# Value and state products issued by half units, and one shared pool for the weight conversions' words and temporaries

## The chip, the cores and the metric

The kernel runs on one core of one Trainium2 chip. Its time is the device time of an execution in microseconds (us). TensorE (PE in the profile; PEld is its weight load) multiplies, VectorE (DVE) and ScalarE (ACT) do the elementwise work and empty PSUM, GpSimd (POOL) does a little, and SyncE (SP) issues nearly all DMA transfers. Each engine works through its own instructions in the order in which they were written.

## The reference, cut to what matters

Three stages follow one another: a linear attention with complex decay, a soft mixture of experts over its output, and a feed-forward layer.

```python
for t in range(S):                          # 768 positions, 4 x 8 heads, head_dim 48
    new_re = ar * S_re - ai * S_im          # a normalised to modulus <= 0.999
    new_im = ar * S_im + ai * S_re
    S_re, S_im = new_re + k[:, :, t] (x) v[:, :, t], new_im
    y[:, :, t] = einsum('bhd,bhde->bhe', q[:, :, t], S_re)
...
logits = x @ phi                            # x: 3072 tokens x 384, 32 slots
slot_input = softmax(logits, 0).T @ x       # over the tokens
h = maximum(slot_input[e] @ w1[e], 0); slot_out[e] = h @ w2[e]      # 8 experts, 384 -> 1024 -> 384
x = softmax(logits, 1) @ slot_out
...
h = x @ w_in                                # 384 -> 2048 -> 384
out = maximum(0.01 * h, h) @ w_out
```

## The kernel before, in words

**Attention.** The work is cut into 12 units: 6 chunks of 128 positions by 2 pairs of batch entries. A unit has 16 heads in two halves (one batch entry each), and four quarters `hq` of 4 heads. Per unit, logarithms, sines and exponentials of the decay are computed (`prep1` to `prep3`, `decay`; their sums over positions are the matmuls of L572), and `prep4` (L625, L634) scales q and k on DVE. Then `attend` writes five steps per quarter:

- `mA` (L649) transposes q and k on PE into a bank of `btr`; ACT or DVE copies them to `qt` and `kt` (L655, L653).
- `mB` (L664) makes the scores in a bank of `bsc`; DVE multiplies them by the causal mask into a tile of `sc` (L667; `sc` has 2 tiles).
- `mC` (L689) adds up scores times v and, from chunk 1 on, q times the carried state `S`, into one bank of `bm` per half. Its matmuls stand in pairs, one writing output partitions 0 to 63 and one 64 to 127. One call covers a quarter: 8 matmuls, or 4 in chunk 0.
- `mD` (L707) makes the quarter's contribution to the state in another bank of `bm`; after the second quarter DVE adds it to `S` and multiplies by the decay (L721, L722; in chunk 0 one instruction, L719). Chunk 5 has no `mD`.
- `mE` copies y out (ACT L730), transposes it (PE L734) and copies it again (ACT L738).

After each chunk, `slots` (L754 to L788) computes the logits and a running softmax sum `acc` over the tokens.

**Experts.** w1 and w2 come as 64 slabs of 384 KB. 49 of them go to tiles of the pool `w`, the others to tiles of other pools that attention has left. `layer1` (L931) and `layer2` (L967) use 32 slabs each, in two groups of experts (`gr`); a group of `layer2` ends with an ACT copy (L974), three transposes (L978) and small DVE copies (L986). `product` (L1004 to L1019) multiplies the result by w_in. A slab can be loaded into a tile of `w` when the earlier owner's last reader is done, and SP issues in order.

**Conversions.** w_in and w_out come as 64-bit floats; `conv` loads a piece of 384 KB into a tile of `raw`, and ACT (L447) and DVE (L448 to L451) narrow it to 32 bits through a tile of `tmp`. There are 16 pieces of w_in and 16 of w_out. For w_out two more instructions split the result (L479, L480).

**Feed-forward.** `ffn1` (L1029 to L1033) and `ffn2` (L1046 to L1048, 1152 matmuls) run to the end.

**What sets the order.** Every step is handed to a planner (`Plan`) with a list of tiles and a cost in us written by hand. The planner simulates the engines with these costs, the pools' numbers of tiles and a few waiting rules, and emits the instructions of each engine in the order that it found. So a changed cost or pool size can move any instruction on any engine.

Of the kernel before, what the change touches and what calls it, by code (L numbers as in the profile page):

```python
# [12 lines left out]
I32 = mybir.dt.int32  # L13
AF = mybir.ActivationFunctionType
ALU = mybir.AluOpType
# [3 lines left out]
B, H, S, D = 4, 8, 768, 48  # L19
# [5 lines left out]
P = 128  # L25
# [3 lines left out]
W = G * D  # L29
# [269 lines left out]
def c_dve(n):  # L299
    return 0.069 + 1.04e-3 * n  # L300
# [19 lines left out]
def tile_kernel(  # L320
# [14 lines left out]
    V, A, GP, T, SY = nc.vector, nc.scalar, nc.gpsimd, nc.tensor, nc.sync  # L335
# [147 lines left out]
    st = [dict() for _ in range(NU)]  # L483
# [154 lines left out]
                    [(q, o), (cs, 0, o), (cs, 1, o)], [d],  # L638
                )

    qt, sc, yb, ub, xt, yt = {}, {}, {}, {}, {}, {}

    def mA(u, hq):
        for nm, tg in (("q", t_qt), ("k", t_kt)):
# [13 lines left out]
    def mB(u, hq):  # L658
        b, t = b_sc(), t_sc([P, 4, P])
        k, q = qt[u, hq, "k"], qt[u, hq, "q"]  # L660

        def mm():
            for i in range(4):
                T.matmul(b()[:, P * i:P * i + P], lhsT=k()[:96, i, :], rhs=q()[:96, i, :], start=True, stop=True)  # L664

        pe(0.88, mm, [k, q], [b])
        dve(c_dve(512), lambda: V.tensor_tensor(t(), b().rearrange("p (i t) -> p i t", t=P), tri.unsqueeze(1).to_broadcast([P, 4, P]), op=ALU.mult), [b], [t])  # L667
        sc[u, hq] = t

    def mC(u, hq):  # L670
        c, bp = divmod(u, 2)
        v = st[u]["v"]
        if hq % 2 == 0:
            yb[u] = b_m()
        y, t, q = yb[u], sc[u, hq], qt[u, hq, "q"]

        def mm():
            for pr in range(2):
                o = P * (2 * (hq % 2) + pr)
                for kind in range(2 if c else 1):  # L680
                    for j in range(2):
                        i = 2 * pr + j
                        g = 4 * hq + i
                        m = 64 if j == 0 and kind == 0 else 48
                        if kind == 0:
                            l, r = v()[:, D * g:D * g + m], t()[:, i, :]
                        else:
                            l, r = sbuf[bp]()[:, D * g:D * g + m], q()[:96, i, :]
                        T.matmul(y()[64 * j:64 * j + m, o:o + P], lhsT=l, rhs=r, start=kind == 0, stop=kind == 1 or c == 0)  # L689

        pe(0.88 if c else 0.44, mm, [t, q, v, (sbuf[bp], hq // 2)], [y])

    def mD(u, hq):
        c, bp = divmod(u, 2)
        if c == NCH - 1:
            return
        s = st[u]
        if hq % 2 == 0:
            ub[u] = b_m()
        b, k, v = ub[u], s["k", hq], s["v"]  # L700

        def mm():
            for i in range(4):
                g = 4 * hq + i
                o = D * (g % 8)
                n = D
                T.matmul(b()[:96, o:o + n], lhsT=k()[:, i].rearrange("p t d -> p (t d)"), rhs=v()[:, D * g:D * g + n], start=True, stop=True)  # L707

        pe(0.68, mm, [k, v], [b])
        if hq % 2 == 1:  # L710
            h = hq // 2
            dc = s["dc"]
            sl = lambda: sbuf[bp]()[:, 8 * D * h:8 * D * h + 8 * D]
            s3 = lambda: sl().rearrange("p (g e) -> p g e", e=D)
            key = (sbuf[bp], h)
            dcb = lambda: dc()[:96, 8 * h:8 * h + 8].unsqueeze(2).to_broadcast([96, 8, D])
            rd = [(dc, 0), (dc, 1)]
            if c == 0:
                dve(c_dve(384), lambda: V.tensor_tensor(s3(), b()[:96, :8 * D].rearrange("p (g e) -> p g e", e=D), dcb(), op=ALU.mult), [b] + rd, [key])  # L719
            else:  # L720
                dve(c_dve(384), lambda: V.tensor_tensor(sl(), b()[:96, :8 * D], sl(), op=ALU.add), [b], [key])  # L721
                dve(c_dve(384), lambda: V.tensor_tensor(s3(), s3(), dcb(), op=ALU.mult), rd, [key])  # L722

    def mE(u, h):
        c, bp = divmod(u, 2)
        bi = 2 * bp + h
        y, b = yb[u], b_m()
        t = yt[c, bi] = t_yt()
        x = xt[c, bi] = t_x()
        act(512, lambda: A.activation(t()[:112], y()[:112, :], AF.Copy), [y], [t])  # L730

        def tr():
            for pr in range(4):
                T.transpose(b()[:, 112 * pr:112 * pr + 112], t()[:112, P * pr:P * pr + P], ident[:112, :112])  # L734

        pe(0.44, tr, [t], [b])
        for j in range(2):
            act(192, lambda j=j: A.activation(  # L738
                x().rearrange("p (r j e) -> p r j e", j=2, e=D)[:, :, j, :],
                b()[:, 0:448].rearrange("p (r w) -> p r w", w=112)[:, :, 64 * j:64 * j + D], AF.Copy), [b], [(x, j)])  # L740

    phi_mm = None

    def slots(c):
# [3 lines left out]
        b, e, lg = (b_sc if last else b_m)(), t_dd(), t_dd()  # L748
        ts = [yt[c, i] for i in range(4)]
# [6 lines left out]
        phi_mm = pe(0.86, mm, ts, [b])  # L756
        m0, m1, n1 = mx[:, c:c + 1], mx[:, c + 1:c + 2], nm[:, c + 1:c + 2]
        dve(0.2, lambda: V.tensor_reduce(m1, b()[:, :P], axis=AX.X, op=ALU.max), [b], [("mx", c + 1)])
        if c:
# [28 lines left out]
            dve(0.2, lambda: V.tensor_reduce(den, e(), axis=AX.X, op=ALU.add), [e], ["den"])  # L788

    def attend(u):  # L790
        for hq in range(4 + 3):
            if hq < 4:
                mA(u, hq)
            if 0 <= hq - 1 < 4:
                mB(u, hq - 1)
            if 0 <= hq - 2 < 4:
                mC(u, hq - 2)
                mD(u, hq - 2)
                if hq % 2 == 1:
                    mE(u, (hq - 2) // 2)  # L800

    turns, done, sel = [], set(), {}

# [347 lines left out]
```

## Time and profile before

| what | value |
|---|---|
| median of 3 runs | 520.32 us (520.12 to 520.55) |
| the profiled execution's own time | 519.7 us |
| its span, first to last instruction | 517.8 us |
| PE busy in the span | 486.8 us (94%), 3985 matmul records |
| DVE busy | 335.4 us (65%) |
| ACT busy | 361.9 us (70%) |
| mean DMA rate | 129 GB/s, 66.97 MB |

The profile is of one execution. A matmul of 32-bit floats appears as two records, and a matmul's record is longer than the distance to the next one, because matmuls overlap. What a run of matmuls costs is therefore read from starts, or from the pieces of the chain of work that ended last. Busy shares are averages over stages with different limits, so the rows further down are given by stage.

### The profile page before, as it was taken

The page shows a single profiled execution, that of the slowest core. Times are in us where ns is not written, and L with a number is a line of the kernel's source. Part 1 is how long each engine was busy: PE and PEld are TensorE (multiplying, and loading weights), DVE is VectorE, ACT ScalarE, POOL GpSimd, SP SyncE. Part 2 cuts the span into 40 slices and gives each one's busy share as a digit, 9 for nine tenths or more (in the row PEclk, how much of TensorE's full clock was granted, in tenths as well). Part 3 has the DMA queues.
Part 4 walks back from the last instruction along what each step waited for, and adds up shares of the span by engine and source line. Part 5 has one row for each costly group of instructions (what it writes and reads, how often), then busy time and mean ns, then how long its engine had stood idle before and what let it go on. Part 6 is the DMA issues. An engine that isn't in the chain of part 4 may idle for free.

```text
span 517.8 us, 10312 instructions
## 1 busy us (share of the span) xinstructions
PE 486.8 (94%) x3985; PEld 433.6 (84%) x3985; DVE 335.4 (65%) x705; ACT 361.9 (70%) x702; POOL 12.7 (2%) x27
## 2 busy tenths in 40 slices
PE   2598979999999999999898999999999999999997
PEld 1387768888889889878553899999999999999997
DVE  4677999999899998997851999825320443025130
ACT  7898999899899999675321799439830994069332
POOL 1000000000000000001000000000000000000000
PEclk9997989999999999999899999999999999999999
DMA  7955245525614746599797234300100110010102
GB/s 266 335 201 154 76 139 155 170 78 154 186 43 143 213 133 231 203 306 305 233 363 308 75 113 121 92 32 17 46 1 0 47 46 1 1 46 2 46 1 91
DMA packets 43844, 66.97 MB, mean 129 GB/s; under 512 B 19098, under 2 KB 24970, under 8 KB 43796
## 3 DMA queue, kind: packets, MB, share of 16 engines
q1 hardware_dynamic: 43476, 66.29, 39.1%
q8 instruction: 31, 0.51, 0.4%
q0 software_dynamic: 320, 0.03, 0.1%
q14 instruction: 17, 0.14, 0.1%
HBM read 61.53 MB, written 4.75 MB: 128 GB/s over the span
## 4 chain that ended last, share of the span: by engine, by line
PE 77%; ACT 9%; DMA 6%; DVE 6%; issue 1%; SPq 0%; POOL 0%; ACTq 0%; DVEq 0%; POOLq 0%
PE b L1047 13%; PE b L1048 13%; PE b L1046 13%; PE btr L649 7%; PE bm L689 6%; PE bsc L664 6%; PE bc L572 5%; PE b L1029 4%; PE bm L707 4%; DMA w<-in_w_dram 3%; ACT L186 2%; DMA raw<-in_wo_dram 1%; PE bm L734 1%; DMA raw<-in_wi_dram 1%; PE b L931 1%
## 5 line engine op out<-in xcount | busy, mean ns | idle before, releaser
L1033 DVE TENSOR_TENSOR w<-x,w 128x384 fp32r<-128x384 f32 x128 | 68.5, 555 | 109.5 <-ACT w L1032 109.5
L1047 PE MATMUL b<-w 128*128 128x384 f32 x384 | 129.2, 337 | 0.3 <-DVE w L1033 0.3
L1046 PE MATMUL b<-w 128*128 128x384 f32 x384 | 128.8, 335 | 0.0
L1048 PE MATMUL b<-w 128*128 128x384 f32 x384 | 128.5, 335 | 0.0
L1032 ACT ACTIVATE w<-x 128x384 fp32r<-128x384 f32 x128 | 63.3, 528 | 19.6 <-PE b L1048 18.4
L1047 PEld LDWEIGHTS b<-w 128*128 128x128 f32 x384 | 72.1, 188 | 0.6 <-DVE w L1033 0.6
L1046 PEld LDWEIGHTS b<-w 128*128 128x128 f32 x384 | 72.1, 188 | 0.0
L1048 PEld LDWEIGHTS b<-w 128*128 128x128 f32 x384 | 72.1, 188 | 0.0
L1031 ACT ACTIVATE x<-b 128x384 f32<-128x384 f32 x128 | 58.8, 491 | 8.6 <-DVE w L1033 5.2
L664 PE MATMUL bsc<-qt,kt 96*128 96x128 f32 x384 | 50.8, 277 | 1.6 <-DVE kt L653 1.0
L1055 ACT ACTIVATE k<-b 128x384 f32<-128x384 f32 x24 | 11.4, 484 | 54.8 <-PE b L1048 54.6
L664 PEld LDWEIGHTS bsc<-qt,kt 96*128 96x128 f32 x384 | 46.2, 192 | 3.2 <-DVE kt L653 1.3
L689 PE MATMUL bm<-sc,w 128*64 128x128 f32 (+1 forms) x384 | 37.4, 281 | 0.3 <-ACT x L738 0.3
L667 DVE TENSOR_TENSOR sc<-bsc,tri_r 128x512 f32<-128x512 f32 x48 | 32.8, 684 | 4.4 <-PE bm L689 2.4
L707 PEld LDWEIGHTS bm<-w,k 128*96 128x96 f32 x320 | 30.9, 167 | 3.2 <-issue 2.2
L707 PE MATMUL bm<-w,k 128*96 128x48 f32 x320 | 33.2, 250 | 0.0
L186 ACT ACT_TABLE_LOAD x25 | 32.1, 1283 | 1.2 <-PEq L1140 0.8
L655 ACT ACTIVATE qt<-btr 96x512 f32<-96x512 f32 x48 | 28.4, 592 | 6.3 <-PE btr L649 5.5
L649 PE MATMUL btr<-ident,q 128*96 128x128 f32 x192 | 30.8, 284 | 1.4 <-DVE q L634 0.8
L689 PE MATMUL bm<-qt,S 96*48 96x128 f32 x320 | 31.2, 272 | 0.0
L649 PE MATMUL btr<-ident,k 128*96 128x128 f32 x192 | 29.9, 281 | 1.1 <-ACT kt L655 0.8
L689 PEld LDWEIGHTS bm<-sc,w 128*64 128x64 f32 (+1 forms) x384 | 21.4, 129 | 8.1 <-issue 4.5
(173 smaller groups left out, 791.8 us busy)
## 6 DMA issues: line engine op xcount, KB each, us to landing
w<-in_w_dram SPq DMA_DIRECT2D x49, 384.0 KB, 5.0
w<-in_qkv_dram SPq DMA_DIRECT2D x36, 384.0 KB, 5.5
w<-in_a_dram SPq DMA_DIRECT2D x22, 384.0 KB, 4.8
raw<-in_wi_dram SPq DMA_DIRECT2D x16, 384.0 KB, 3.3
raw<-in_wo_dram SPq DMA_DIRECT2D x16, 384.0 KB, 3.1
out_dram<-k SPq DMA_DIRECT2D x24, 192.0 KB, 1.8
cs<-in_w_dram SPq DMA_DIRECT2D x6, 384.0 KB, 5.4
k<-in_w_dram SPq DMA_DIRECT2D x6, 192.0 KB, 3.8
```

Of the source, the lines that this page charges most:

```text
L186: self.preload(TABLES[name])
L649: T.transpose(b()[:96, P * i:P * i + P], src()[:, i].rearrange("p t d -> p (t d)"), ident)
L664: T.matmul(b()[:, P * i:P * i + P], lhsT=k()[:96, i, :], rhs=q()[:96, i, :], start=True, stop=True)
L667: dve(c_dve(512), lambda: V.tensor_tensor(t(), b().rearrange("p (i t) -> p i t", t=P), tri.unsqueeze(1).to_broadcast([P, 4, P]), op=ALU.mu ...
L689: T.matmul(y()[64 * j:64 * j + m, o:o + P], lhsT=l, rhs=r, start=kind == 0, stop=kind == 1 or c == 0)
L707: T.matmul(b()[:96, o:o + n], lhsT=k()[:, i].rearrange("p t d -> p (t d)"), rhs=v()[:, D * g:D * g + n], start=True, stop=True)
L1031: act(NG, lambda: A.activation(u(), b()[:, :NG], AF.Prelu, alpha=0.01), [b], [u])
L1032: act(NG, lambda: A.activation(g()[:, 0], u(), AF.Copy), [u], [(g, 0)])
L1033: dve(c_dve(NG), lambda: V.tensor_tensor(g()[:, 1], u(), g()[:, 0].bitcast(F32), op=ALU.subtract), [u, (g, 0)], [(g, 1)])
L1046: T.matmul(b()[:, :DM], lhsT=lh, rhs=wh()[:, i], start=f == FO[0], stop=False)
L1047: T.matmul(b()[:, :DM], lhsT=ll, rhs=wh()[:, i], start=False, stop=False)
L1048: T.matmul(b()[:, :DM], lhsT=lh, rhs=wl()[:, i], start=False, stop=f == FO[-1])
```

## The change

`mC` and `mD` are called once per half unit in place of once per quarter, so that 16 (chunk 0: 8) and 8 matmuls stand in one step that the planner can't cut. `mD` writes to a bank of `bsc` in place of `bm`. The costs given to the planner are new (2.0 and 1.13 for `mC`, 1.36 for `mD`, 1.15 for the logits' matmuls). The pools `raw` and `tmp` with 2 tiles each are gone, their users take tiles of `w`, and `w` has 33 tiles in place of 29; the memory taken is the same.

```diff
-    t_w = Tag(mem, "w", [P, W], 29)
+    t_w = Tag(mem, "w", [P, W], 33)
...
-    t_raw = Tag(mem, "raw", [P, W // 2, 2], 2, I32)
-    t_tmp = Tag(mem, "tmp", [P, 2, W // 2], 2)
...
     def conv(src, i, dst):
 
-        raw = t_raw()
+        raw = t_w([P, HW, 2], I32)
...
-        tmp = t_tmp()
+        tmp = t_w([P, 2, HW])
...
-    def mC(u, hq):
+    def mC(u, h):
+
         c, bp = divmod(u, 2)
-        v = st[u]["v"]
-        if hq % 2 == 0:
-            yb[u] = b_m()
-        y, t, q = yb[u], sc[u, hq], qt[u, hq, "q"]
+        v, hs = st[u]["v"], (2 * h, 2 * h + 1)
+        y = yb[u] = b_m()
...
-        pe(0.88 if c else 0.44, mm, [t, q, v, (sbuf[bp], hq // 2)], [y])
...
+        pe(2.0 if c else 1.13, mm, [x for hq in hs for x in (sc[u, hq], qt[u, hq, "q"])] + [v, (sbuf[bp], h)], [y])
...
-        if hq % 2 == 0:
-            ub[u] = b_m()
-        b, k, v = ub[u], s["k", hq], s["v"]
+        b, v, ks = b_sc(), s["v"], [s["k", 2 * h + j] for j in range(2)]
...
-        pe(0.68, mm, [k, v], [b])
...
+        pe(1.36, mm, ks + [v], [b])
...
     def attend(u):
-        for hq in range(4 + 3):
+        for hq in range(5):
             if hq < 4:
                 mA(u, hq)
-            if 0 <= hq - 1 < 4:
+            if hq:
                 mB(u, hq - 1)
-            if 0 <= hq - 2 < 4:
-                mC(u, hq - 2)
-                mD(u, hq - 2)
-                if hq % 2 == 1:
-                    mE(u, (hq - 2) // 2)
+            if hq in (2, 4):
+                mC(u, hq // 2 - 1)
+                mD(u, hq // 2 - 1)
+                mE(u, hq // 2 - 1)
```

**TensorE, behind the second chunk's slot sums** (at 116 us in the trace of before). `sc` are masked scores, `w` is v, `qt` is q, `S` the state; the numbers tell tiles apart. Before:

```order
L777 MATMUL bm_1409<-x_1365,dd_1399 32x384
L689 MATMUL bm_1420<-sc_1300,w_609 64x128
L689 MATMUL bm_1420<-sc_1300,w_609 48x128
L689 MATMUL bm_1420<-qt_1178,S_396 48x128 x2
...
L649 MATMUL btr_1434<-ident_60,q_1385 96x128 x4
L649 MATMUL btr_1439<-ident_60,k_1401 96x128 x4
L689 MATMUL bm_1420<-sc_1363,w_609 64x128
L689 MATMUL bm_1420<-sc_1363,w_609 48x128
L689 MATMUL bm_1420<-qt_1193,S_396 48x128 x2
```

The same place now:

```order
L771 MATMUL bm_1412<-x_1300,dd_1405 32x384
L688 MATMUL bm_1420<-sc_1357,w_578 64x128
L688 MATMUL bm_1420<-sc_1357,w_578 48x128
L688 MATMUL bm_1420<-qt_1188,S_396 48x128 x2
...
L688 MATMUL bm_1420<-sc_1379,w_578 64x128
L688 MATMUL bm_1420<-sc_1379,w_578 48x128
L688 MATMUL bm_1420<-qt_1247,S_396 48x128 x2
...
L662 MATMUL bsc_1446<-qt_1364,kt_1369 128x128 x4
```

The two transposes that stood between the two quarters' products have moved behind them. Over the whole program, matmuls of `mC` stand in 41 runs before (4 of 4, 32 of 8, 5 of 16 matmuls) and in 24 now (4 of 8, 20 of 16); of chunks 1 to 5 alone, in 35 and 20. Runs of `mD` go from 34 to 20.

**SyncE, the last loads before the feed-forward.** `in_w_dram` are slabs, `in_wi_dram` and `in_wo_dram` pieces to convert. Before:

```order
L352 DMA x<-in_w_dram 128x384 x3
L352 DMA raw<-in_wi_dram 128x768
L352 DMA raw<-in_wo_dram 128x768
L352 DMA w<-in_w_dram 128x768 x20
L352 DMA raw<-in_wo_dram 128x768 x15
```

Now:

```order
L352 DMA qt<-in_w_dram 128x384 x2
L352 DMA x<-in_w_dram 128x384 x3
L352 DMA w<-in_w_dram 128x768 x16
L352 DMA w<-in_wo_dram 128x768 x16
```

Four slabs have moved ahead of the last run of slabs, the last piece of w_in has moved up among the earlier loads, and the first piece of w_out has moved behind the slabs.

**TensorE, the end of the experts' second layer.** Before:

```order
L967 MATMUL b<-k,h_91 32x384 x3
L967 MATMUL b<-qt,h_91 32x384
L978 MATMUL b<-ident,x 128x128 x3
L967 MATMUL b<-w,h_91 32x384 x16
L978 MATMUL b<-ident,x 128x128 x3
```

Now:

```order
L960 MATMUL b<-k,h_91 32x384 x3
L960 MATMUL b<-qt,h_91 32x384
L960 MATMUL b<-w,h_91 32x384 x8
L971 MATMUL b<-ident,x 128x128 x6
```

The transposes of the first group of experts no longer stand ahead of the last matmuls of the second group, and half of those 16 matmuls stand earlier.

On VectorE, conversion instructions (L448 to L451) ahead of the last unit's phase step (L584 there, L582 now) go from 36 to 48 of the 64 for w_in; the other 16 follow before the feed-forward in place of 28.

## Rows read from the trace of the kernel before

**Rows 1.** Head of the page.
```profile
span 517.8 us, 10312 instructions
```

**Rows 2.** Windows: stretch and length, busy us (instructions) per engine, clock, DMA.
```profile
66.00:216.00 150.00, 147.29 (x1525) 126.39 (x1524) 141.29 (x264) 137.94 (x224) 6.03 (x8) 0.99 0.49 151
216.00:255.12 39.12, 35.56 (x405) 29.27 (x405) 35.19 (x93) 24.52 (x52) 2.63 (x6) 1.00 0.84 277
255.12:285.19 30.07, 28.07 (x345) 13.98 (x345) 11.89 (x50) 5.41 (x10) 0.70 (x2) 0.94 0.88 322
285.19:517.80 232.61, 229.04 (x1350) 226.62 (x1350) 99.08 (x206) 136.06 (x316) 0.00 (x0) 1.00 0.14 43
```

**Rows 3.** Chain that ended last, 78 to 118 us: shares by line.
```profile
by line: PE bm L689 23.0%; PE btr L649 19.8%; PE bsc L664 18.5%; PE bm L707 14.6%; PE bc L572 13.5%; PE bm L777 3.9%; PE bm L734 3.9%; PE bm L754 2.5%; PE bm L768 0.3%; PE bm L769 0.3%
```

**Rows 4.** The same chain's pieces: start us, length us, engine, line, records.
```profile
88.70 0.64 PE bm L707 x8
89.33 0.44 PE btr L649 x4
89.78 1.02 PE bm L689 x15
90.80 0.81 PE bm L707 x8
...
92.63 0.57 PE btr L649 x4
```

**Rows 5.** Pieces of the chain, 168 to 216 us.
```profile
169.84 1.90 PE bm L689 x31
171.74 1.49 PE bm L707 x16
```

**Rows 6.** Waits of 66 to 216 us: total us, times, longest us.
```profile
DVE sc L667 <- PE bm L689: 2.4, 3, 1.5
```

**Rows 7.** Groups by line: busy us, mean ns of one, idle before.
```profile
L450 DVE SCALAR_TENSOR_TENSOR tmp<-raw,tmp 128x384 int32<-128x384 int32 x32 | 17.6, 554 | 0.4
L449 DVE TENSOR_SCALAR tmp<-tmp 128x384 int32<-128x384 int32 x32 | 11.1, 357 | 0.5
L448 DVE TENSOR_SCALAR tmp<-tmp 128x384 f32<-128x384 f32 x32 | 11.1, 354 | 7.5 <-ACT tmp L447 7.5
L451 DVE SCALAR_TENSOR_TENSOR wi<-raw,tmp 128x384 int32<-128x384 int32 x16 | 8.6, 550 | 0.0
```

**Rows 8.** Timeline of SP's issues: start us, length us of merged issues.
```profile
257.78 16.74 SPq L352 DMA_DIRECT2D w<-in_w_dram  x20
275.18 23.47 SPq L352 DMA_DIRECT2D raw<-in_wo_dram  x6
```

**Rows 9.** Windows: the stretch of the last slabs; columns as in rows 2.
```profile
257.80:282.90 25.10, 24.28 (x319) 11.93 (x310) 8.19 (x36) 3.48 (x7) 0.70 (x2) 0.98 0.96 360
```

**Rows 10.** Timeline of PE in the experts' stage; idle time before in brackets.
```profile
269.56 1.50 PE L967 MATMUL b<-w,h 128*32 128x384 f32 x16
270.99 0.66 PE L942 MATMUL b<-ident,kt 128*128 128x128 f32 x4
...
274.18 1.47 PE L967 MATMUL b<-cs,h 128*32 128x384 f32 x16
275.47 1.47 PE L967 MATMUL b<-w,h 128*32 128x384 f32 x16
...
278.93 0.55 PE L978 MATMUL b<-ident,x 128*128 128x128 f32 x3 [0.70 <-ACT x L974]
279.41 4.06 PE L967 MATMUL b<-w,h 128*32 128x384 f32 x32
284.14 0.55 PE L978 MATMUL b<-ident,x 128*128 128x128 f32 x3 [0.67 <-ACT x L974]
285.19 2.80 PE L1004 MATMUL b<-wi,so 128*32 128x256 f32 x48 [0.50 <-DVE so L986]
```

**Rows 11.** Timeline of ACT: the first late conversion of w_out.
```profile
282.89 0.55 ACT L447 ACTIVATE tmp<-raw 128x384 f32<-128x384 f32 x1 [4.01 <-DMA raw<-in_wo_dram]
```

More of the change, by code (lines that the diff above doesn't have):

```diff
@@ L639, in prep4 @@
                 )
-    qt, sc, yb, ub, xt, yt = {}, {}, {}, {}, {}, {}
+    qt, sc, yb, xt, yt = {}, {}, {}, {}, {}
     def mA(u, hq):
@@ L664, in mm, with mD @@
                 T.matmul(b()[:, P * i:P * i + P], lhsT=k()[:96, i, :], rhs=q()[:96, i, :], start=True, stop=True)
-        pe(0.88, mm, [k, q], [b])
+        pe(0.9, mm, [k, q], [b])
         dve(c_dve(512), lambda: V.tensor_tensor(t(), b().rearrange("p (i t) -> p i t", t=P), tri.unsqueeze(1).to_broadcast([P, 4, P]), op=ALU.mult), [b], [t])
         sc[u, hq] = t
-    def mC(u, hq):
+    def mC(u, h):
         c, bp = divmod(u, 2)
-        v = st[u]["v"]
-        if hq % 2 == 0:
-            yb[u] = b_m()
-        y, t, q = yb[u], sc[u, hq], qt[u, hq, "q"]
+        v, hs = st[u]["v"], (2 * h, 2 * h + 1)
+        y = yb[u] = b_m()
         def mm():
[L678 to L689, printed above, removed]
-        pe(0.88 if c else 0.44, mm, [t, q, v, (sbuf[bp], hq // 2)], [y])
-    def mD(u, hq):
+            for hq in hs:
+                t, q = sc[u, hq], qt[u, hq, "q"]
+                for pr in range(2):
+                    o = P * (2 * (hq % 2) + pr)
+                    for kind in range(2 if c else 1):
+                        for j in range(2):
+                            i = 2 * pr + j
+                            g = 4 * hq + i
+                            m = 64 if j == 0 and kind == 0 else 48
+                            if kind == 0:
+                                l, r = v()[:, D * g:D * g + m], t()[:, i, :]
+                            else:
+                                l, r = sbuf[bp]()[:, D * g:D * g + m], q()[:96, i, :]
+                            T.matmul(y()[64 * j:64 * j + m, o:o + P], lhsT=l, rhs=r, start=kind == 0, stop=kind == 1 or c == 0)
+        pe(2.0 if c else 1.13, mm, [x for hq in hs for x in (sc[u, hq], qt[u, hq, "q"])] + [v, (sbuf[bp], h)], [y])
+    def mD(u, h):
         c, bp = divmod(u, 2)
@@ L697, in mD @@
         s = st[u]
-        if hq % 2 == 0:
-            ub[u] = b_m()
-        b, k, v = ub[u], s["k", hq], s["v"]
+        b, v, ks = b_sc(), s["v"], [s["k", 2 * h + j] for j in range(2)]
         def mm():
[L703 to L707, printed above, removed]
-        pe(0.68, mm, [k, v], [b])
-        if hq % 2 == 1:
[L711 to L722, printed above, removed]
+            for i in range(8):
+                g = 8 * h + i
+                T.matmul(b()[:96, D * i:D * i + D], lhsT=ks[i // 4]()[:, i % 4].rearrange("p t d -> p (t d)"), rhs=v()[:, D * g:D * g + D], start=True, stop=True)
+        pe(1.36, mm, ks + [v], [b])
+        dc = s["dc"]
+        sl = lambda: sbuf[bp]()[:, 8 * D * h:8 * D * h + 8 * D]
+        s3 = lambda: sl().rearrange("p (g e) -> p g e", e=D)
+        key = (sbuf[bp], h)
+        dcb = lambda: dc()[:96, 8 * h:8 * h + 8].unsqueeze(2).to_broadcast([96, 8, D])
+        rd = [(dc, 0), (dc, 1)]
+        if c == 0:
+            dve(c_dve(384), lambda: V.tensor_tensor(s3(), b()[:96, :8 * D].rearrange("p (g e) -> p g e", e=D), dcb(), op=ALU.mult), [b] + rd, [key])
+        else:
+            dve(c_dve(384), lambda: V.tensor_tensor(sl(), b()[:96, :8 * D], sl(), op=ALU.add), [b], [key])
+            dve(c_dve(384), lambda: V.tensor_tensor(s3(), s3(), dcb(), op=ALU.mult), rd, [key])
     def mE(u, h):
@@ L754, in mm @@
                     T.matmul(b()[32 * i:32 * i + 32, :P], lhsT=phi[:, pr, :], rhs=ts[i]()[:112, P * pr:P * pr + P], start=pr == 0, stop=pr == 3)
-        phi_mm = pe(0.86, mm, ts, [b])
+        phi_mm = pe(1.15, mm, ts, [b])
         m0, m1, n1 = mx[:, c:c + 1], mx[:, c + 1:c + 2], nm[:, c + 1:c + 2]
```

1 line of the change is left out of this document (removed).

## The prediction, made before the changed kernel ran

> **What bounds the kernel now.** I read the busy time by stage first, since a mean over the whole program mixes limits. Four stretches cover nearly all of it [rows 2]. From 66 to 216 us (attention with its pipeline full) PE is busy 147.29 of 150 us, DVE 141.29, ACT 137.94: three engines near their limit. From 216 to 255.12 us attention runs out and the experts' slabs stream in; DMA is at 0.84. From 255.12 to 285.19 us the experts run, DMA at 0.88. From 285.19 us on only the feed-forward is left, with PE busy 229.04 of 232.61 us.
>
> Which of the three full engines bounds attention is told by the chain of work that ended last: between 78 and 118 us it holds nothing but PE, 23.0% of it in the products of L689 [rows 3]. So a microsecond taken off PE there is worth something until DVE, which has 150 - 141.29 = 8.7 us to spare in 150, takes over.
>
> In the experts' stage the last run of 20 slabs is issued from 257.78 us on, and the pieces of w_out queue behind them from 275.18 us [rows 8]; DMA is at 0.96 and moves 360 GB/s [rows 9]. PE must have the last slabs before it can start the product at 285.19 us [rows 10].
>
> **The change, part by part.**
>
> *The runs of value products.* No matmul is removed. What a run costs beside its matmuls is in the chain's pieces. A quarter's 8 matmuls take 1.02 us; two quarters that already stand together take 1.90, so the second saves 0.14 [rows 4, 5]. The piece behind a run is longer too: four transposes take 0.57 us behind one and 0.44 elsewhere (0.13 more), a quarter of `mD` 0.81 and 0.64 (0.17 more) [rows 4]. An avoided run is thus worth 0.27 to 0.31 us. In chunks 1 to 5 the order goes from 35 runs to 20: 15 x 0.27 to 0.31 = 4.1 to 4.7 us. In chunk 0, outside the stretches read here, two runs fewer would bring at most 0.6 us; I count nothing. I take 4.2 us less work for PE, of which some 3.7 lies before 216 us and 0.5 behind it (3 of 24 half units).
>
> *The runs of state products.* Two quarters of `mD` together take 1.49 us behind a value run, apart 0.81 + 0.64 = 1.45 [rows 4, 5]. Nothing.
>
> The Trainium skill has a rule for the extra time at both ends of a run: by TensorEngine Tiling, Tiling Modes (Key Properties), a change of the array's tiling mode drains TensorE, and `mC` is the step that writes in two column halves. By TensorE: Matmul & The Clock Gate, Single matmul latency, a drain is about 0.175 us, so with two per run the estimate from that page would be 15 x 0.35 = 5.3 us in place of 4.2. The rows are of this kernel and of the same pairs of steps, and they decide.
>
> *How much of it arrives.* DVE gets more to do in the same stretch. Twelve more conversion instructions stand ahead of the last unit's phase step, three of each of four kinds: 3 x (0.354 + 0.357 + 0.554 + 0.550) = 5.4 us [rows 7]. The order shows other DVE work (q and k products, state updates) going the other way past the same mark, 0.55 to 0.84 us each; counting the rows of each kind ahead of the mark in both orders gives a net of about 3 us more. DVE would then be busy 144.3 us of 150 - 3.7 = 146.3, that is 98.6%, against 94.2% before. Both ends: if every gap of DVE closes, all 3.7 us arrive; if DVE needs its old 8.7 us of gaps, the stretch takes 144.3 + 8.7 = 153 us and loses 3. I take 2.2 us, a little over the middle of 0 and 3.7, because DVE's waits for PE in this stretch are short: the largest kind for a value run is 2.4 us in three waits [rows 6], and a conversion fits into such a gap. Behind 216 us DVE loses those 5.4 us, PE its 0.5; I take 0.5. Together attention ends 2.7 us earlier.
>
> *The scores' banks.* `mD` now holds one of two `bsc` banks until its addition to `S`, and that waits for the value run of the same half. The price lies between nothing and the rival below; I take nothing in the sum, as part of the 1.5 us that I hold back.
>
> *The last slabs.* Four of the last 20 slabs are issued before the experts start, where DMA has room (0.84). 4 x 0.393 MB at 360 GB/s is 4.4 us [rows 9], so the last slab lands that much earlier after the experts' start. PE then sets the pace. Records of L967 are issued 16 in 275.47 - 274.18 = 1.29 us when slabs are there [rows 10]. All 128 from 269.56 us on take 10.3 us, with four transposes of L942 between (270.99 to about 271.55, 0.6): 280.5 us. Before, the last 32 records began at 279.41, behind the first group's transposes (0.70 us idle, then 0.55), and took 4.06 us where 2.58 would do: they ended at 283.47. From there to the product it was 285.19 - 283.47 = 1.72 us; with six transposes at the end in place of three I take 2.0. The product starts at 282.5 in place of 285.19: 2.7 us. With DMA's 4.4 us the last slabs are there in time, by about 2 us. Bounds: nothing, if the four slabs find no tile free before the experts start; 4.4, if all that DMA gains were on the path.
>
> *The first piece of w_out.* It was loaded ahead of the 20 slabs and now comes behind 16. It lands one transfer (1.1 us) behind the last slab, near 282.9 - 4.4 + 1.1 = 279.6 us on the old clock. Its conversion is about 3.5 us (0.55 of ACT [rows 11], 1.82 of DVE [rows 7], two more instructions of this size), so it is ready at 283.1; the feed-forward's second layer can't begin before the product's 2.80 us are over, 285.3 [rows 10]. Cost nothing, hidden by the product; if that cover were gone, the excess over 2.2 us of delay would stand in front of the feed-forward.
>
> *Feed-forward.* The same 1152 matmuls, PE full [rows 2]; four more tiles can only loosen it. Nothing.
>
> Sum: 2.7 + 2.7 = 5.4 us. The profiled execution took 519.7 us, 1.9 more than its span [rows 1], so 514.3; the median of the runs lies 0.6 above that execution, which gives 514.9 us.
>
> **The rivals.** A difference of 0.2% (1.0 us) is about what this measurement can tell from none; slower means above 521.4, faster below 519.3.
>
> 1. *DVE takes over.* All of PE's saving in attention is lost because DVE has no room for the conversions; the experts still gain 2.7: 517.6 us. For it: 98.6% is close to full. Against it: DVE's work is the same in total, and the planner now has PE costs near the rows (2.0 for 1.90, where 0.88 stood for 1.02). The Trainium skill says the same in general: TensorEngine Tiling, Performance Considerations (PSUM Bottleneck), warns that faster matmuls leave the evacuation by ACT and DVE as the limit; in this trace both are at 92% or more between 66 and 216 us. Chance 0.20.
> 2. *The slabs gain nothing.* Their four tiles come free only at attention's end: attention's 2.7 alone, 517.6 us. For it: the tiles of `w` are shared with v and the conversions. Against: the order has all of w_in's loads ahead of them. Chance 0.08.
> 3. *Everything arrives.* 4.7 from PE, 0.6 from chunk 0 and up to 4.4 from DMA: 510.6 us. Against it: PE paces the second layer. Chance 0.10.
> 4. *The long run starves DVE (slower).* A run of 1.90 us holds both `sc` tiles and, through the state addition, a `bsc` bank, 0.88 us longer than a quarter's; no mask product and no next scores can pass. In the 16 half units with a state product that is up to 14.1 us more waiting on DVE. DVE can absorb 8.7 - 3 = 5.7 us, so full price is 8.4 us against a slab gain of 2.7: 526.0 us. It decides from (5.7 + 2.7)/16 = 0.53 us per half unit on. For it: DVE already waits 2.4 us for L689 in front of mask products [rows 6]. Against: only three such waits in 150 us, and transposes and sums stand between most runs. Chance 0.16.
> 5. *It does nothing:* within 0.2%. Chance 0.05.
>
> My own forecast has the remaining 0.41, from 512 to 517 us.
>
> **How the numbers follow.** Faster: 0.41 + 0.20 + 0.08 + 0.10 = 0.79; I give 0.01 of it to each of the others, since rivals 1 and 2 together would be no change: 0.77, 0.06, 0.17. For the range I leave out the slower rival (0.16) and the outermost part of rival 3: 511.2 to 521.2 us.
>
> **What would show it.** Right: single runs of 32 value records near 1.90 us on the chain; PE's work per chunk about 0.8 us shorter; the experts' start near 252.4 us; the 128 second-layer records in about 11 us without a pause; the product 27.4 us after the experts' start; the feed-forward's length unchanged. Wrong: DVE idle for PE's value or state products by more than 8 us in attention, PE waiting for mask products or for a `bsc` bank, slabs landing after PE asks for them, or the first second-layer matmul waiting for a converted piece of w_out.

## The result and the profile after

The changed kernel took 513.85 us (median of 4 runs, 512.20 to 515.49) beside 520.22 us (4 runs) of the kernel before: a ratio of 0.9875, 95% interval 0.9842 to 0.9909. It was measured a second time, beside 17 other runs of the kernel before (518.70 us): 514.61 us (6 runs, 514.20 to 516.09), ratio 0.9925, interval 0.9903 to 0.9946. So it is faster by 4.1 to 6.4 us; 514.9 us, or a ratio of 0.9896, was predicted.

Part of the larger figure is probably TensorE's clock, whose granted mean differs from one execution to the next. Of the 17 runs of the kernel before, those at 0.987 to 0.990 took 518.7 to 520.4 us, those at 0.996 and 0.997 only 517.4 to 517.9. In the second measurement the mean is 0.992 for both kernels, and runs of both at 0.993 lie 3.4 us apart (medians 517.59 and 514.23). In the first, the changed kernel's four ran at 0.997; the clocks of the runs beside it are not on record. So 3.4 to 4.1 us is the better figure for the change itself.

There are two profiles of the changed kernel, one from each measurement: executions of 515.49 and 516.09 us, both the longest of their sets. The marks of the prediction (us; the last row is a kernel of the experiments whose order is nearly the same up to the product):

| execution | its time | last logits' matmul | experts' start | start to product | product to second layer | second layer to end |
|---|---|---|---|---|---|---|
| before | 519.70 | 247.91 | 255.12 | 30.07 | 5.81 | 226.80 |
| after, first profile | 515.49 | 244.51 | 252.19 | 27.44 | 7.11 | 226.86 |
| after, second profile | 516.09 | 242.76 | 251.76 | 28.52 | 7.10 | 226.82 |
| product due earlier (below) | 513.48 | 243.2 | 251.0 | 27.1 | 7.3 | 226.2 |

The head and the busy times of the page of the first profile, and its chain of work that ended last, by engine:

```profile
span 513.6 us, 10264 instructions
...
PE 480.4 (94%) x3985; PEld 433.8 (84%) x3985; DVE 330.5 (64%) x705; ACT 357.5 (70%) x702; POOL 13.0 (3%) x27
...
PE 66%; DVE 19%; ACT 7%; DMA 4%; issue 2%; SPq 1%; POOL 0%; ACTq 0%; DVEq 0%; POOLq 0%
```

PE is busy 6.4 us less in all, with the same matmuls; some of it is the clock, which fell in attention before and not after (last section). The chain now runs through DVE for 19% of the span; before, it was 6%:

```profile
PE 77%; ACT 9%; DMA 6%; DVE 6%; issue 1%; SPq 0%; POOL 0%; ACTq 0%; DVEq 0%; POOLq 0%
```

Windows of the first profile, cut at the same events as [rows 2] (stretch and length, busy us and instructions of PE, PEld, DVE, ACT and POOL, clock, DMA share, GB/s):

```profile
66.00:216.00 150.00, 145.74 (x1538) 128.19 (x1540) 147.09 (x282) 142.35 (x236) 6.71 (x8) 1.00 0.53 161
216.00:252.19 36.19, 33.29 (x406) 28.84 (x403) 30.63 (x82) 19.99 (x46) 2.27 (x6) 1.00 0.87 310
252.19:279.63 27.44, 26.72 (x344) 13.90 (x344) 7.08 (x39) 4.28 (x9) 0.70 (x2) 0.94 0.91 341
279.63:513.60 233.97, 229.18 (x1350) 225.93 (x1350) 98.45 (x212) 133.90 (x317) 0.00 (x0) 1.00 0.11 36
```

From 66 us to the experts' start PE is busy 147.29 + 35.56 - 145.74 - 33.29 = 3.8 us less than in [rows 2]; DVE, busy 141.29 us before, is now the fullest engine up to 216 us, with 147.09 of 150 (98%). But the stretch to 216 us now holds more of the program. Up to the last unit's phase step, at 214.37 us before and at 210.40 and 208.66 in the two profiles after, DVE's work has hardly grown, by 1.0 to 1.1 us:

```profile
0.00:214.37 214.37, 192.47 (x1871) 162.45 (x1873) 187.64 (x357) 195.44 (x324) 9.32 (x19) 0.98 0.53 168
```
```profile
0.00:210.40 210.40, 185.66 (x1835) 159.89 (x1836) 188.78 (x364) 194.68 (x324) 10.01 (x19) 1.00 0.56 174
```
```profile
0.00:208.66 208.66, 184.27 (x1835) 158.33 (x1836) 188.64 (x364) 194.61 (x324) 10.00 (x19) 1.00 0.55 175
```

The experts' stage is 2.6 us shorter, the feed-forward's stretch 233.97 - 232.61 = 1.4 us longer.

Pieces of the chain that answer to [rows 5]: a whole half unit's value products as one run, and state products as one.

```profile
178.92 1.32 PE bsc L703 x16
180.24 1.90 PE bm L688 x31
...
191.94 1.90 PE bm L688 x31
```

The waits of 66 to 250 us (total us, times, longest us) that answer to [rows 6]: no mask product waits for a value run any more. PE now waits for a `bsc` bank four times, 2.4 us together: three state products (L703) until a mask product has read the bank, one score product until a state addition has. The kernel before shows no such wait.

```profile
PE bsc L703 <- DVE sc L665: 1.6, 3, 0.7
DVE sc L665 <- PE bsc L662: 1.5, 1, 1.5
...
PE bsc L662 <- DVE S L715: 0.8, 1, 0.8
```

The last loads on SP's timeline, which answer to [rows 8]:

```profile
254.63 13.21 SPq L352 DMA_DIRECT2D w<-in_w_dram  x16
268.47 43.16 SPq L352 DMA_DIRECT2D w<-in_wo_dram  x16
```

PE's timeline from the end of the experts on, which answers to [rows 10]:

```profile
276.42 1.47 PE L960 MATMUL b<-w,h 128*32 128x384 f32 x16
277.82 0.55 PE L971 MATMUL b<-ident,x 128*128 128x128 f32 x3
278.59 0.55 PE L971 MATMUL b<-ident,x 128*128 128x128 f32 x3 [0.23 <-ACT x L967]
279.63 2.80 PE L997 MATMUL b<-wi,so 128*32 128x256 f32 x48 [0.49 <-DVE so L979]
...
284.23 0.69 PE L1022 MATMUL b<-q,qt 128*128 128x384 f32 x3
...
285.23 0.75 PE L1022 MATMUL b<-q,qt 128*128 128x384 f32 x3
286.74 0.44 PE L1039 MATMUL b<-w 128*128 128x384 f32 x1 [0.76 <-ACT x L1024]
```

The second layer of the experts ends at 277.82 without the 0.70 us pause that stood at 278.93 before. The one thing lost is at the end: the first layer of the feed-forward (L1022) begins 4.60 us behind the product's start, where it was 3.78, and the second layer (L1039) then waits 0.76 us for ScalarE to empty a bank. The first layer's first call before, with the product at 285.19:

```profile
288.97 0.71 PE L1029 MATMUL b<-q,qt 128*128 128x384 f32 x3
```

### The profile page after: what moved, and what is told of

It is laid out like the page before. It is cut to its first block, busy times and chain, and to the rows that moved or that the text cites. A ratio compares the mean times of both kernels' runs of the same rounds, so it can differ in the third digit from the quotient of the medians.

```text
span 513.6 us, 10264 instructions
## 1 busy us (share of the span) xinstructions
PE 480.4 (94%) x3985; PEld 433.8 (84%) x3985; DVE 330.5 (64%) x705; ACT 357.5 (70%) x702; POOL 13.0 (3%) x27
## 4 chain that ended last, share of the span: by engine, by line
PE 66%; DVE 19%; ACT 7%; DMA 4%; issue 2%; SPq 1%; POOL 0%; ACTq 0%; DVEq 0%; POOLq 0%
PE b L1039 13%; PE b L1040 13%; PE b L1041 13%; PE b L1022 4%; PE bsc L662 4%; PE bm L688 4%; PE btr L647 3%; PE b L924 2%; DVE sc L665 2%; PE bc L570 2%; DVE k L632 2%; PE bsc L703 2%; PE b L960 2%; DVE q L632 2%; DVE w L526 2%
## 5 line engine op out<-in xcount | busy, mean ns | idle before, releaser
L1039 PE MATMUL b<-w 128*128 128x384 f32 x384 | 128.6, 335 | 0.8 <-ACT x L1024 0.8
L1039 PEld LDWEIGHTS b<-w 128*128 128x128 f32 x384 | 72.1, 188 | 1.0 <-ACT x L1024 1.0
L662 PE MATMUL bsc<-qt,kt 96*128 96x128 f32 x384 | 52.6, 283 | 1.8 <-DVE S L715 0.8
L688 PE MATMUL bm<-sc,w 128*64 128x128 f32 (+1 forms) x384 | 36.3, 277 | 0.1
L647 PE MATMUL btr<-ident,q 128*96 128x128 f32 x192 | 30.3, 281 | 1.9 <-ACT qt L653 1.0
L703 PEld LDWEIGHTS bsc<-w,k 128*96 128x96 f32 x320 | 29.0, 165 | 3.4 <-DVE sc L665 2.5
L703 PE MATMUL bsc<-w,k 128*96 128x48 f32 x320 | 30.3, 247 | 1.6 <-DVE sc L665 1.6
L647 PEld LDWEIGHTS btr<-ident,q 128*96 128x96 f32 x192 | 21.5, 130 | 6.4 <-ACT qt L653 1.7
```

Of the source, the lines that this page charges most:

```text
L647: T.transpose(b()[:96, P * i:P * i + P], src()[:, i].rearrange("p t d -> p (t d)"), ident)
L703: T.matmul(b()[:96, D * i:D * i + D], lhsT=ks[i // 4]()[:, i % 4].rearrange("p t d -> p (t d)"), rhs=v()[:, D * g:D * g + D], start=True, ...
L1039: T.matmul(b()[:, :DM], lhsT=lh, rhs=wh()[:, i], start=f == FO[0], stop=False)
```

## The experiments

The theory at the start: attention gains because fewer value runs cost PE less, and the experts' stage gains because the shared pool lets four slabs be issued earlier. Rivals: either gain comes from the planner's new costs alone, or from the other part of the change; and the bank of `mD` matters. Ratios are to the kernel before, run beside each.

**1. The pool alone:** quarters, banks and costs of before, with the pools changed.

```diff
-    t_w = Tag(mem, "w", [P, W], 29)
+    t_w = Tag(mem, "w", [P, W], 33)
-    t_raw = Tag(mem, "raw", [P, W // 2, 2], 2, I32)
-    t_tmp = Tag(mem, "tmp", [P, 2, W // 2], 2)
...
-        raw = t_raw()
+        raw = t_w([P, HW, 2], I32)
```

> The quarters stay; only the conversions' tiles move to the pool of 33. The last run of slabs has 13 in place of 20. Theory A (fewer value runs shorten attention, the pool shortens the experts' stage): the experts start at 254 to 256 us as before (255.1), the stretch from there to the product shrinks from 30.1 to about 27.4 us, the feed-forward begins 1.3 us later after the product as in the changed kernel; time 517 to 519 us. Rival C (the pool is what shortens attention, since conversions no longer wait for two raw tiles): experts start near 252 us, time about 515.

Measured: 520.07 us, 1.0018 (1.0002 to 1.0033). The experts' start is at 256.1 us and the stage takes 30.1 us, as before. SP's timeline and PE's:

```profile
264.46 10.92 SPq L352 DMA_DIRECT2D w<-in_w_dram  x13
```
```profile
280.90 1.81 PE L965 MATMUL b<-w,h 128*32 128x384 f32 x4 [0.15 <-DMA w<-in_w_dram]
282.89 1.48 PE L965 MATMUL b<-w,h 128*32 128x384 f32 x10 [0.18 <-DMA w<-in_w_dram]
```

The second layer begins 6.35 us behind the product. Theory A's shorter stage didn't come, nor rival C's early start. Only 13 slabs are left for the last run, but it begins 8.4 us behind the experts' start, because SP stood before loads into `S`, `qt`, `x` and `w` in between, and PE waits for slabs at the end. The number of slabs in the last run says nothing without its start.

**2. The half units alone:** the changed kernel with `raw`, `tmp` and 29 tiles of `w` put back.

```diff
-    t_w = Tag(mem, "w", [P, W], 33)
+    t_w = Tag(mem, "w", [P, W], 29)
+    t_raw = Tag(mem, "raw", [P, W // 2, 2], 2, I32)
+    t_tmp = Tag(mem, "tmp", [P, 2, W // 2], 2)
...
-        raw = t_w([P, HW, 2], I32)
+        raw = t_raw()
```

> Half units with own pools for the conversions and w of 29. Theory A: experts start near 252 us, the stretch to the product stays at 30 us, the feed-forward starts as before; time about 517 us. Rival C: experts start near 255 us, time 520. If the two parts add up, the savings of this kernel and of the pool alone sum to that of the whole change, 6.4 us.

Measured: 517.78 us, 0.9978 (0.9954 to 1.0002). Experts' start 255.7, stage 30.0, product to second layer 5.8: the stages of before. That is theory A's time with rival C's start. The two parts together bring 4.1 to 6.4 us, apart +0.9 and -1.4 (the interval of the second just reaches no change): they do not add.

**3. Pool and costs, with quarters:** the changed kernel with `mC` and `mD` called per quarter again, `mD` in `bm`, and the new costs halved for them. The cost of the scores' matmuls, 0.90 in the changed kernel where it was 0.88, is new here too.

```diff
-    def mC(u, h):
+    def mC(u, hq):
...
-        pe(2.0 if c else 1.13, mm, [x for hq in hs for x in (sc[u, hq], qt[u, hq, "q"])] + [v, (sbuf[bp], h)], [y])
+        pe(1.0 if c else 0.565, mm, [t, q, v, (sbuf[bp], hq // 2)], [y])
...
-        b, v, ks = b_sc(), s["v"], [s["k", 2 * h + j] for j in range(2)]
+        if hq % 2 == 0:
+            ub[u] = b_m()
```

> Pool of 33, value and state products by quarters as before, but the planner is told the higher costs (1.0 and 0.565 a quarter of value products, 1.15 for the logits). 37 value runs in place of 24. Theory A: PE has about 13 x 0.27 = 3.5 us more work than in the changed kernel and the experts start at 254.5 to 256 us; time 517 to 519. Rival B (it is the planner's better order, not the runs): experts start near 252 us and the time is within 1 us of the changed kernel's 514.

Measured: 519.51 us, 1.0005 (0.9985 to 1.0025). The stage takes 25.7 us, the shortest of all, with the changed kernel's last loads, and at the full clock:

```profile
258.06 11.88 SPq L352 DMA_DIRECT2D w<-in_w_dram  x16
```
```profile
256.58:282.33 25.75, 25.03 (x345) 13.00 (x345) 7.08 (x39) 4.27 (x9) 0.70 (x2) 1.00 0.96 357
```

It is the changed kernel's stage without the clock that this one lost: 27.44 us less 1.7 in the first profile, 28.52 less 2.8 in the second. The ten profiles here whose second layer runs without a pause all have 25.7 us left in this way, and the layer's 128 records start within 10.8 us in each, where they took 13.4 before.

The stage starts at 256.6, 1.5 us later than before, and the feed-forward's second layer begins 7.1 us behind the product. So the experts' gain needs the pool and the new costs, not the half units; without them attention ends no earlier than before in this profile.

**4. The state products in their old bank:** one line of the changed kernel.

```diff
-        b, v, ks = b_sc(), s["v"], [s["k", 2 * h + j] for j in range(2)]
+        b, v, ks = b_m(), s["v"], [s["k", 2 * h + j] for j in range(2)]
```

> The changed kernel with the state products in a bank of bm in place of bsc. If the shared score banks cost nothing (my sum): within 1 us of the changed kernel, 513 to 515. If holding a score bank until the state addition costs (the mechanism of the slower rival, in part): faster by over 1 us, with no waits of PE for VectorE in front of scores or state products. If bm is the scarcer one: slower, with waits for ScalarE's copies of y.

Measured: 518.92 us, 1.0003 (0.9982 to 1.0024): the gain is gone. Experts' start 255.7, stage 28.4. The value runs are as few as in the changed kernel (24) and PE is busy 143.52 us from 66 to 216 us, less than there. The waits of 66 to 256 us that are new:

```profile
PE bc L570 <- ACT w L607: 4.6, 4, 1.6
PE bsc L662 <- ACT kt L653: 1.7, 2, 1.2
```

PE saves work and then waits for ScalarE, not for a bank and not for copies of y: the planner has put the steps in another order.

**5 and 6. The price of a run.** `mC` and `mD` of a half unit in one step of the planner, once with the value products first (24 value runs), once with a quarter of each in turn (44). The planner sees the same steps and costs in both, so all else stands in the same order.

In turn, the state products inside the loop over quarters; in the other kernel both quarters' state products stand behind it:

```diff
-            for hq in hs:
+            for n, hq in enumerate(hs):
...
+                if has:
+                    state(n)
...
-        pe(1.36, mm, ks + [v], [b])
```

> A half unit's value and state products are one step for the planner, value products first (one run of 16, then 8). It is the base for the next kernel. Both theories: within 2 us of the changed kernel.

> The same step with the same cost, so the same order of everything else; inside it the quarters alternate (8 value, 4 state, 8 value, 4 state). Only the number of value runs differs: 16 more of 8 in chunks 1 to 4, 4 more in chunk 0. Theory A: 0.27 to 0.31 us each, 4.3 to 5 us more work on PE in chunks 1 to 4; where PE is the limit the time grows by that, where VectorE has taken over by less, 2 to 5 us together. Rival B: no difference over 0.5 us.

Measured: 519.28 us, 0.9990 (0.9974 to 1.0006), and 522.05 us, 1.0043 (1.0021 to 1.0065). One half unit on PE's timeline, value products first:

```profile
178.45 0.43 PE L696 MATMUL bm<-sc,w 128*64 128x128 f32 x4
...
180.35 1.56 PE L680 MATMUL bsc<-w,k 128*96 128x48 f32 x16
181.75 0.60 PE L647 MATMUL btr<-ident,q 128*96 128x128 f32 x4
```

And in turn:

```profile
180.29 0.43 PE L696 MATMUL bm<-sc,w 128*64 128x128 f32 x4
...
183.86 0.60 PE L647 MATMUL btr<-ident,q 128*96 128x128 f32 x4
```

From the first value product to the transposes behind: 181.75 - 178.45 = 3.30 us against 183.86 - 180.29 = 3.57. So a run more costs PE 0.27 us, in 19 of the 20 half units that differ (0.01 in the other), the lower end of what the prediction read from [rows 4, 5]. It is the price of the cut in the state products too, which goes with it. Nineteen of them are 5.1 us of PE's work; the time grew by 522.05 - 519.28 = 2.8 us (1.7 to 3.5 by the means), 0.14 per run. About half of what PE saves arrives. But kernel 5, with as few runs as the changed kernel, starts its experts at 256.6 us: few runs alone don't bring the 2.9 us.

**7 and 8. Is DVE the limit?** Three of the four DVE instructions of each piece of w_in are left out, in the changed kernel and in the kernel before (w_in's values are wrong); the order of all else is kept.

```diff
-        dve(c_dve2(n), lambda: V.tensor_scalar(t1(), t1(), 2.0 ** -15, None, op0=ALU.max), [], [k1])
+        dve(c_dve2(n), lambda: short or V.tensor_scalar(t1(), t1(), 2.0 ** -15, None, op0=ALU.max), [], [k1])
...
```

> The changed kernel with the planned order kept, but three of the four VectorE instructions of each w_in piece are left out (the final one reads the raw words), so w_in's values are wrong and 48 x about 0.42 us = 15 us of VectorE work in attention is gone. If VectorE is what limits 66 to 216 us now: the last unit's phase step comes 2 to 4 us earlier than 210.4 us. If PE still limits it: less than 1 us.

> The same omission in the kernel before, its order kept. There PE limited attention: the last unit's phase step stays within 1 us of 214.4 us. If VectorE limited it too, it comes earlier by as much as in the changed kernel. The difference between the two short kernels at that step is then what the runs are worth to PE, 3 to 4 us.

Measured: 513.74 us, 0.9880 (0.9842 to 0.9918), and 518.00 us, 0.9965 (0.9950 to 0.9981). Windows of the changed kernel so shortened:

```profile
66.00:216.00 150.00, 146.29 (x1567) 129.84 (x1566) 136.57 (x251) 143.14 (x237) 6.55 (x8) 1.00 0.52 165
```

DVE has lost 10.5 us there. The last unit's phase step comes at 207.7 us, 2.7 us earlier than in the first profile of the changed kernel, which looked like a DVE limit, but only 0.9 earlier than in the second, whose order is the same. Counted from the first logits' matmul, the difference is clear: to the phase step it is 146.76 and 146.73 us in the two profiles of the changed kernel, 146.73 and 146.72 in kernels 10 and 11, and 145.88 here; to the last logits' matmul 180.82 to 180.86 and 179.97. So 10.5 us of DVE's work are worth 0.9 us of attention, and the ratio can't be told from the changed kernel's two. By the expectation's terms PE still limits, at DVE 98% busy; ACT (143.14) and PE (146.29) stand right behind it, which would explain it. In the kernel before, where DVE was at 94%, the omission brings 0.35% (0.2 to 0.5), 1.8 us: no less. Its phase step comes at 213.7 us, within 1 us as expected. But the two shortened kernels lie 6.0 us apart there, not the 3 to 4 that the runs were to be worth: the runs are not all that changed.

**9. The changed kernel again**, for a second profile.

> The changed kernel once more, for a second profile beside other kernels on one chip. If the 7.1 us from the product to the first matmul of the feed-forward's second layer belong to the order of the instructions, they stand here again (7.0 to 7.2), with 210 to 211 us for the last phase step, 252 us for the experts' start and 27.4 us from there to the product; the time is 512.5 to 515. If they belong to that one execution, this profile shows about 5.8 and a time near 512.5.

Measured: 514.61 us; the marks are in the table. The 7.1 us repeat to 0.01. The phase step stands at 208.7, not at 210 to 211, and the experts' stage is a microsecond longer, for which the clock speaks (last section).

**10. w_out's conversions shortened** in the changed kernel, as in 7 (w_out's values are wrong).

> The changed kernel with three of the four VectorE conversion instructions of every piece of w_out left out (w_out's values are wrong); the order of everything else is the same. Theory: after the product VectorE and ScalarE meet the first conversions of w_out between the product's copies and those of the first layer, and that is what puts 7.1 us where 5.8 stood. Then the stretch from the product to the second layer falls to 5.8 to 6.3 us, the experts' start stays at 252 us, and the time is 0.8 to 1.3 us below the changed kernel's. Rival: the first piece of w_out or the tiles that it needs come late, whatever VectorE does; then the stretch stays at 7.0 or more and the time within 0.4 us. A second rival: the order of PE and ScalarE alone sets it (four more product pieces ahead of the first layer's first call); then it stays at about 6.8.

Measured: 514.85 us, 0.9927 (0.9906 to 0.9948). PE's timeline at the two ends of the stretch:

```profile
279.54 2.80 PE L997 MATMUL b<-wi,so 128*32 128x256 f32 x48 [0.49 <-DVE so L979]
...
284.13 0.68 PE L1022 MATMUL b<-q,qt 128*128 128x384 f32 x3
...
286.63 0.44 PE L1039 MATMUL b<-w 128*128 128x384 f32 x1 [0.76 <-ACT x L1024]
```

7.09 us, with the same wait: the theory that VectorE's conversions stand in the way falls. The second rival, PE's and ScalarE's own order, is left.

**11 and 12. Other due times.** The planner is told that the product is due 4 us earlier, and in 12 the first layer's first four calls too (the second pair of lines, which 11 lacks).

```diff
+    plan.lead = 4.0
     product()
+    plan.lead = 0.0
...
+    plan.lead = 4.0
     for f in FO[:ahead]:
         for j in range(2):
             ffn1(j, f)
+    plan.lead = 0.0
```

> The changed kernel with the planner told that the product's steps are due 4 us earlier; up to the product almost the same order, and from there some conversions of w_out behind the product's copies. If the conversions cost the 1.3 us, the stretch from the product to the second layer falls by 0.3 to 1.0 us and the time by as much; if PE's own order sets it, nothing moves (within 0.3 us).

> The same for the product and for the first four calls of the feed-forward's first layer. Theory: the stretch from the product to the second layer is 5.8 to 6.3 us. The planner moves attention's steps too, so the experts' start may move by up to 2 us either way: if it stays at 252 us, the time is about 1 us below the changed kernel's, and this is the fastest version; if the start goes later by more than 1 us, nothing is won. Rival: the stretch stays at 7 us, and the time is that of the changed kernel plus the shift of the start.

Measured: 514.01 us (513.17 to 514.78), 0.9914 (0.9893 to 0.9935), and 514.84 us, 0.9944 (0.9920 to 0.9968). In 11 the second layer's first matmul comes 7.3 us behind the product, but the product is 233.5 us from the end in place of 233.9 to 234.0. In 12 the first call of the first layer stands behind eight of the product's small matmuls again, as before, and not behind twelve (one call there, where the kernel before had three):

```profile
284.49 2.80 PE L997 MATMUL b<-wi,so 128*32 128x256 f32 x48 [0.49 <-DVE so L979]
...
288.44 0.37 PE L1022 MATMUL b<-q,qt 128*128 128x384 f32 x1
...
290.55 0.44 PE L1039 MATMUL b<-w 128*128 128x384 f32 x1
```

6.06 us, no wait for a bank, and 232.3 us from the product to the end, with all conversions in place: this points to the order of the first layer's calls as the cause of the loss. But the planner moved other steps, attention's among them, as well, and nothing was won. The experts' start is at 257.4 us in this profile, an execution of 518.75 us; nine of its twelve runs took 513.24 to 515.53. Not all of that start is the order's, since this trace lost 5.1 us of clock between 69 and 79 us, for instance here:

```profile
70.00:74.00 4.00, 4.00 (x24) 3.97 (x23) 3.13 (x6) 3.98 (x7) 0.00 (x0) 0.50 0.37 103
```

Kernel 11 has the lowest time of these, 0.6 us below the changed kernel beside it; the ranges of the two overlap, so a gain isn't shown.

The planner's order held fixed while only a bank or a pool changes, which would have separated the order from the resources, was not tried.

## Why the prediction was right, and where it was not

The forecast, faster by 1.0%, was right in direction, and the measured 4.1 and 6.4 us lie on both sides of the 5.4 us that it added up; most of its sum came true, one term failed, and the clock, which it left out, helped in places. Point by point:

- **Fewer value runs make PE's work 4.2 us shorter:** right. PE is busy 3.8 us less from 66 us to the experts' start, of which up to 1.7 can be the lower clock before near 70 us; in the shortened pair (8 and 7), whose traces lose none there, it is 4.4. The price of a run, taken from the chain at 0.27 to 0.31 us, was measured by itself at 0.27 (experiments 5 and 6). The Trainium skill's rule (TensorEngine Tiling, Tiling Modes: a mode change drains TensorE; TensorE: Matmul & The Clock Gate, Single matmul latency) gave an estimate of 0.35 per run; the runs here say 0.27 of PE's work and 0.14 of time.
- **2.7 us of it arrive at the experts' start:** right in size (2.9 in the first profile, 3.4 in the second), wrong in place. 2.2 were to arrive before 216 us. The last but one of the logits' matmuls, at 220.2 us before, starts at 220.3 and 218.5; the last one, at 247.9, at 244.5 and 242.8. So 0 to 1.7 us are won by then and 3.5 between the two. There PE works 2.3 us less and its 1.2 us of idle time are gone. Conversions on DVE don't explain it: they fall from 14 to 9 instructions in this stretch, and experiment 8 has 4.3 us less of them there than the kernel before, for 0.7 us of time. The three, in this order (before, first profile after, experiment 8):

```profile
220.22:247.91 27.69, 26.49 (x304) 22.29 (x303) 24.48 (x57) 17.14 (x37) 2.11 (x5) 1.00 0.87 288
```
```profile
220.27:244.51 24.24, 24.16 (x296) 21.58 (x295) 20.91 (x49) 12.82 (x31) 1.77 (x5) 1.00 0.88 316
```
```profile
219.56:246.58 27.02, 26.23 (x304) 22.29 (x303) 20.77 (x47) 17.03 (x37) 1.56 (x5) 1.00 0.88 296
```

- **DVE's extra work:** sized too high. About 3 us more were counted ahead of the last unit's phase step; it is 1.0 to 1.1.
- **Why they arrive is only half shown.** The measured 0.14 us per run gives 15 x 0.14 = 2.1 us for the avoided runs. But kernels with the same 24 runs start their experts at 255.7 (2, 4) and 256.6 us (5), and quarters with pool and costs, in 37 runs, at 256.6 (3). Of all orders with few runs only that of the whole change starts them at 250 to 252 (7, 9, 10, 11). The planner orders every engine anew for each set of costs, pools and banks, and what it did better in this one order stays open.
- **The scores' banks cost nothing:** not quite. PE waits 2.4 us for them, and that these waits stand on the path isn't shown. And nothing was not the value of the step: with `mD` in `bm` the gain is gone (4). The prediction priced the bank's occupancy and not what the planner does with it.
- **The last slabs, 2.7 us:** right in its steps, 16 slabs, no pause in the second layer, six transposes at the end; that it was 2.63 in the first profile is luck in part. That profile and the one of the kernel before both lost 1.7 us of clock in the stage. The second profile lost 2.8 and gains 1.55. Where no clock is lost, the stage takes 25.7 us with the last slabs early (3) and 30.1 to 30.3 with them late (1, 8), so there the step is worth about 4.5. Its condition was missing too: the pool alone gives nothing (1), where SP's queue is held by other loads.
- **The first piece of w_out, nothing:** this step failed. The stretch from product to second layer grew by 1.3 us, in every profile of this order. It did not fail as the prediction feared, by a late piece: shortened conversions change nothing (10). What the runs leave is the order of the first layer's calls, which changed there and which the prediction did not read: four more small matmuls stand ahead of the first call, and a bank comes free later. Kernel 12, with eight of them there, needs 6.06 us.
- **Feed-forward, nothing:** right, 226.8 and 226.9 us from its second layer's first matmul.
- **Rivals.** DVE did become the fullest engine, as rival 1 says, but taking 10.5 us of its work away brings 0.9 us of attention (7): it doesn't eat the gain. The Trainium skill's warning that evacuation becomes the limit (TensorEngine Tiling, Performance Considerations) fits the 98%, not the price. Rival 4's sign, mask products waiting for value runs, is absent; PE's waits for a `bsc` bank, which the prediction named among the signs of being wrong, are there, but short.

The sum for the first profile is 2.93 + 2.63 - 1.30 - 0.06 = 4.2 us, the difference of the two spans. The gain of the first measurement's medians, 6.4 us, is larger, since that execution is the longest of its four and, as said above, the clock has a part in it.

## What to carry to other kernels

A saving on one engine is worth what the next two engines leave of it: with three at 92% to 98%, half of PE's saving arrived, and DVE's own work, taken away, brought less than a tenth. Before a stage's length is put down to its order, take off the clock that it lost: the experts' stages of 25.7, 27.4 and 28.5 us are the same work. Where a planner decides the order, undoing one part of a change does not price that part; a pair of kernels that the planner sees as the same, such as 5 and 6, does. When a step moves, read the order of every engine up to the next full stage: the one lost microsecond stood where only the moved transfer had been looked at.

## What the runs showed of the hardware

The granted clock differed between executions of the same instructions. Windows of 4 us of the second profile of the changed kernel, and of the first:

```profile
244.00:248.00 4.00, 2.51 (x18) 1.61 (x20) 3.49 (x17) 1.81 (x7) 0.00 (x0) 0.90 1.04 385
248.00:252.00 4.00, 2.79 (x18) 1.58 (x14) 1.47 (x5) 0.44 (x2) 0.00 (x0) 0.50 0.50 153
252.00:256.00 4.00, 4.00 (x40) 2.07 (x36) 1.39 (x5) 0.36 (x1) 0.00 (x0) 0.50 0.14 44
256.00:260.00 4.00, 4.00 (x61) 2.31 (x54) 0.00 (x0) 0.60 (x1) 0.00 (x0) 0.82 0.94 309
```
```profile
248.00:252.00 4.00, 2.59 (x18) 1.48 (x18) 2.48 (x10) 1.67 (x7) 0.00 (x0) 1.00 0.65 231
252.00:256.00 4.00, 3.81 (x40) 2.50 (x44) 1.79 (x7) 0.36 (x1) 0.00 (x0) 0.57 0.37 107
256.00:260.00 4.00, 4.00 (x68) 2.62 (x64) 0.04 (x1) 0.60 (x1) 0.00 (x0) 1.00 0.83 274
```

PE is less busy where attention ends, and the clock then falls to the lower of its levels (0.50 is 1.2 of 2.4 GHz). Added up, the missing parts are 4 x (0.10 + 0.50 + 0.50 + 0.18) = 5.1 us in the one, some 10 us at half clock, and 4 x 0.43 = 1.7 us in the other. Behind the experts' start, at 251.76 and 252.19 us, lie 2.8 and 1.7 of them, which fits stages of 28.5 and 27.4 us. In the kernel before the clock also fell near 70 us, and around 44:

```profile
44.00:48.00 4.00, 4.00 (x27) 3.90 (x26) 2.74 (x6) 3.55 (x7) 0.00 (x0) 0.62 1.00 323
64.00:68.00 4.00, 2.33 (x15) 1.56 (x14) 3.94 (x7) 3.97 (x7) 0.00 (x0) 0.94 0.86 321
68.00:72.00 4.00, 3.80 (x17) 3.02 (x17) 3.01 (x7) 2.91 (x5) 0.76 (x1) 0.63 0.03 6
```

In the changed kernel's two profiles it stayed at 1.00 there, and so it did in those of kernels 7, 10 and 11, which have its order in attention. Whether the order brings that about isn't shown. The dip near 70 can have cost before at most 4 x 0.37 + 4 x 0.06 = 1.7 us, which would be part of attention's gain. The earlier one was over before the first logits' matmul, which starts no later there (61.3 us) than after (63.6 and 61.9), or in experiment 8 (62.1), whose trace lost only half as much clock there.
